# Float64 weights to float32 in three VectorE instructions, and the softmax norm fused with the float16 split

## The chip, the cores and the metric

One NeuronCore of one Trainium2 chip runs the whole program. The metric is the device time of one launch in microseconds (us), from the first to the last instruction on that core. Its engines are TensorE (PE; the loading of its weights is listed apart as PEld), VectorE (DVE), ScalarE (ACT), GpSimd (POOL) and SyncE (SP). SP computes nothing here: it issues every DMA of the kernel.

## The reference

An attention with a window of 128 keys, then two gated blocks on its output. Everything is float32, except that the weights of the two blocks arrive as float64.

```python
# q, k, v: [4, 8, 576, 64]; 8 heads, 576 positions
scores = q @ k^T / 8 - slope[h] * |i - j|, kept for 0 <= i - j < 128
attn = exp(scores - max(scores)); attn = attn / (sum(attn) + 1e-9)
x = (attn @ v)                       # as [2304, 512]
x = ((x @ w_a) * (x @ w_b)) @ w_out      # 512 -> 1536 -> 512
y = ((x @ w1) * (x @ w2)) @ w3 @ w_out2  # 512 -> 1024 -> 1024 -> 512
```

## The kernel before

**Products.** A float32 product is three float32r passes on PE: each operand is split into hi = float32r(x) and lo = x - hi (`split`, L138). The attention's probabilities and v are split in another way, into float16 and bfloat16 parts.

**Weights.** Each piece of a weight (a *part*, 128 x 512 values) is loaded by SP as float64, that is as two 32-bit words for each value (tile `raw`). `convert` (L98) makes float32 of it in stages. Stage s0 takes the absolute value of the high word on ACT (L107). Stage s1 is five DVE instructions: clear what is too small and make a mask (L113), shift and mask (L117), put sign and top bit in (L120), take the exponent (L123), and weigh the low word with it (L127). Stage s3 adds the two on POOL (L132). Then `split` makes hi on ACT (L139) and lo on POOL (L73). There are 76 parts. The tile `ca` holds the value, and the tile `ce`, of which there is one, what comes from the low word; `ce` is also the staging buffer of the product w3 @ w_out2 (L440 to L442). The class `Stages` puts a part's stages into the program in turns, one stage of every live part a turn.

**Attention.** 16 units (a batch and a pair of heads) of 5 query blocks each make 80 steps. A step: scores on PE (L313), bias and minimum on DVE (L325, one for each head), exp with its sum on ACT (L331), sum to reciprocal on DVE (L344, L347), then `probs` (L349): scale by the reciprocal on DVE in place (L357, one for each head), round to float16 on ACT (L363; on DVE, L361, for the first block of a unit), subtract that for the low part on POOL (L73), transpose both parts by a DMA that SP issues (L366), and the product with v on PE (L388) eight steps later. Blocks 1 to 3 of a unit have two heads with 256 keys, block 0 two heads with 128, block 4 one tile of 256.

**After attention.** Ten groups of gated products (L521 and L541 or L559), each with six parts of weights, and 24 parts for the product w3 @ w_out2 between them. From some 285 us on the weights of a group are converted while PE works on the one before.

**Order.** The program is traced through a tile scheduler: it fixes each engine's order of instructions, places the waits, and gives a tile's buffer to the next user when its last reader is through. An engine runs its list in order, so an instruction that waits holds all behind it.

Of the kernel before, what the change touches and what calls it, by code (L numbers as in the profile page):

```python
# [20 lines left out]
# Float32 products run as three float32r passes: an operand x is the exact sum of  # L21
# hi = float32r(x) and lo = x - hi, and x*w = lo*hi' + hi*lo' + hi*hi' to float32's accuracy.
# The second block's w3 @ w_out is formed first: (g @ w3) @ w_out = g @ (w3 @ w_out).
# Weights come as float64: their words are put together as rounded float32 on the chip.
# [6 lines left out]
GROUPS = (6, 4)  # groups of two 128-column chunks of each block's inner features  # L31
TA, TN = 256, 512  # tokens of a tile: beside attention, and after it
HALF = 1280  # the token at which the accumulators are cut in two
LAG, NLAG = 8, 2  # steps of attention from the scores to the product with v, and to the norms
AT = (0, 0, 1, 3)  # steps of a unit at which the next one is transposed
V_AT = {2: 1, 6: 2}  # steps at which the second and the third unit's v are loaded
FILL = 0.75  # microseconds of the first group's products in a step of attention
PACE = (0.3, 0.6)  # turns of the weights' conversion in a step: the first batch, the others
TURN = 400  # tokens of a chunk for each turn later
# [4 lines left out]
def attention_moe_moe(ctx, tc, q, k, v, w_a, w_b, w_o, w_1, w_2, w_3, w_o2, out):  # L44
# [34 lines left out]
    # ---------------------------------------------------------------- weights  # L79
    def load_cols(w, c):  # L80
        """128 columns of a [512, .] weight: [128, 4 * 128] with the rows on 4 x 128 partitions."""
# [7 lines left out]
    def load_rows(w, r, c):  # L89
        """128 rows and 512 columns."""  # L90
# [7 lines left out]
    def convert(raw, hi=None, lo=None, use=()):  # L98
        """Float64's two words as float32, to the nearest (0 below float32's exponents), and its
        split: stages, to be emitted one after the other, each when the one before has run."""  # L100
# [5 lines left out]
        def s0():  # L106
            nc.scalar.activation(a, f32(hw), ACTF.Abs)  # L107

        def s1():
            e = pools["conv"].tile([P, W], F32, name="ce", bufs=1)  # L110
            ei = e.bitcast(I32)
            es.append(e)
            nc.vector.tensor_scalar(  # L113
                out=a, in0=a, scalar1=bits(0x38100000), scalar2=bits(0x3FFFFFF8),
# [639 lines left out]
```

## Time and profile before

| | us |
|---|---|
| median of 3 runs | 1056.13 (1048.25 to 1060.08) |
| profiled execution, first to last instruction | 1056.7 |
| PE busy | 1017.9 (96%) |
| DVE busy | 691.0 (65%) |
| POOL busy | 494.3 (47%) |
| ACT busy | 382.0 (36%) |

The profiled execution has no time of its own beside its span; the span is 0.6 us above the median of the runs. Busy PE is not PE at its peak: its matmuls are pipelined and a waiting one can count as busy. PE's granted clock is a share of 2.4 GHz; 0.5 is 1.2 GHz. A group of instructions is listed as line, engine, operation, out<-in, shape, count | busy us, mean ns of one | idle us of the engine before them and what ended it.

### The profile page before, as it was taken

The page shows a single profiled execution, that of the slowest core. Times are in us where ns is not written, and L with a number is a line of the kernel's source. Part 1 is how long each engine was busy: PE and PEld are TensorE (multiplying, and loading weights), DVE is VectorE, ACT ScalarE, POOL GpSimd, SP SyncE. Part 2 cuts the span into 40 slices and gives each one's busy share as a digit, 9 for nine tenths or more (in the row PEclk, how much of TensorE's full clock was granted, in tenths as well). Part 3 has the DMA queues.
Part 4 walks back from the last instruction along what each step waited for, and adds up shares of the span by engine and source line. Part 5 has one row for each costly group of instructions (what it writes and reads, how often), then busy time and mean ns, then how long its engine had stood idle before and what let it go on. Part 6 is the DMA issues. An engine that isn't in the chain of part 4 may idle for free.

```text
span 1056.7 us, 16482 instructions
## 1 busy us (share of the span) xinstructions
PE 1017.9 (96%) x6162; PEld 838.2 (79%) x6162; DVE 691.0 (65%) x1420; ACT 382.0 (36%) x929; POOL 494.3 (47%) x409
## 2 busy tenths in 40 slices
PE   7889999999999889999999999999999999999998
PEld 5567788787987778887788788888888888888886
DVE  6999997757499995587969659565273373322222
ACT  5555766655344232332333323233322221211110
POOL 6566645445267562264636226477572352421111
PEclk9688979878899899999999999999999999999999
DMA  6867676656333221232232223121021020000012
GB/s 140 170 122 154 118 114 121 123 101 115 81 100 100 79 100 70 74 107 73 99 109 84 77 71 99 60 80 41 1 80 40 20 81 20 20 1 1 11 70 100
DMA packets 160080, 85.23 MB, mean 81 GB/s; under 512 B 128000, under 2 KB 148992, under 8 KB 160000
## 3 DMA queue, kind: packets, MB, share of 16 engines
q1 hardware_dynamic: 160000, 84.18, 31.5%
q8 instruction: 48, 0.79, 0.3%
q14 instruction: 32, 0.26, 0.1%
HBM read 58.20 MB, written 8.91 MB: 64 GB/s over the span
## 4 chain that ended last, share of the span: by engine, by line
PE 62%; DVE 22%; DMA 6%; issue 6%; ACT 2%; POOL 1%; SPq 1%; DVEq 0%; ACTq 0%; POOLq 0%
PE mm L521 33%; PE mm L559 10%; PE mm L541 7%; DVE ca L117 4%; PE tr L388 4%; PE mm L439 4%; PE s L313 3%; DVE pe L357 3%; DVE ca L120 3%; DVE ca L113 2%; DVE ce L123 2%; DMA pt<-pp 2%; DVE ce L127 2%; DMA raw<-in_moe_w_out 1%; DVE pe L325 1%
## 5 line engine op out<-in xcount | busy, mean ns | idle before, releaser
L73 POOL TENSOR_TENSOR gl<-g,gh 128x512 fp32r<-128x512 f32 (+1 forms) x108 | 127.7, 1183 | 265.3 <-ACT gh L531 258.4
L132 POOL TENSOR_TENSOR ca<-ca,ce 128x512 f32<-128x512 f32 x76 | 104.7, 1378 | 138.2 <-DVE ce L127 127.4
L528 DVE TENSOR_TENSOR g<-a,mm 128x512 f32<-128x512 f32 (+1 forms) x108 | 64.1, 594 | 157.3 <-PE mm L521 146.7
L531 ACT ACTIVATE gh<-g 128x512 fp32r<-128x512 f32 (+1 forms) x108 | 60.4, 559 | 209.4 <-DVE g L528 209.1
L73 POOL TENSOR_TENSOR pp<-pe,pp 128x512 f16<-128x512 f32 (+1 forms) x80 | 81.8, 1030 | 73.1 <-ACT pp L363 39.9
L521 PE MATMUL mm<-x_hi,wlA 128*128 128x512 f32 (+1 forms) x464 | 109.2, 356 | 0.0
L521 PE MATMUL mm<-x_lo,whA 128*128 128x512 f32 (+1 forms) x464 | 106.9, 351 | 0.0
L521 PE MATMUL mm<-x_hi,whA 128*128 128x512 f32 (+1 forms) x464 | 106.2, 349 | 0.0
L521 PE MATMUL mm<-x_hi,wlB 128*128 128x512 f32 (+1 forms) x400 | 99.8, 371 | 5.5 <-DVE g L528 5.0
L526 ACT ACTIVATE a<-mm 128x512 f32<-128x512 f32 (+1 forms) x108 | 56.1, 519 | 126.6 <-PE mm L521 126.5
L521 PE MATMUL mm<-x_lo,whB 128*128 128x512 f32 (+1 forms) x400 | 98.8, 369 | 0.0
L521 PE MATMUL mm<-x_hi,whB 128*128 128x512 f32 (+1 forms) x400 | 98.7, 369 | 0.0
L521 PEld LDWEIGHTS mm<-x_lo,whA 128*128 128x128 f32 x464 | 80.3, 197 | 10.5
L521 PEld LDWEIGHTS mm<-x_hi,whA 128*128 128x128 f32 x464 | 79.7, 196 | 11.1
L113 DVE TENSOR_SCALAR ca<-ca 128x512 f32<-128x512 f32 x76 | 48.8, 642 | 60.4 <-ACT ca L107 60.4
L521 PEld LDWEIGHTS mm<-x_hi,wlA 128*128 128x128 f32 x464 | 78.6, 195 | 12.1 <-issue 0.6
L107 ACT ACTIVATE ca<-raw 128x512 f32<-128x512 f32 x76 | 50.9, 669 | 101.5 <-DMA raw<-in_moe_w 51.6
L521 PEld LDWEIGHTS mm<-x_hi,wlB 128*128 128x128 f32 x400 | 70.6, 188 | 19.9 <-DVE g L528 6.1
L117 DVE SCALAR_TENSOR_TENSOR ca<-raw,ca 128x512 int32<-128x512 int32 x76 | 82.4, 1084 | 1.6
L357 DVE TENSOR_SCALAR pe<-pe,st 128x256 f32<-128x256 f32 (+1 forms) x144 | 81.5, 602 | 1.3
L331 ACT ACTIVATE pe<-pe,st 128x256 f32<-128x256 f32 (+1 forms) x144 | 68.7, 478 | 37.6 <-DVE st L325 36.0
L120 DVE SCALAR_TENSOR_TENSOR ca<-raw,ca 128x512 int32<-128x512 int32 x76 | 80.9, 1065 | 1.5
(100 smaller groups left out, 2086.7 us busy)
## 6 DMA issues: line engine op xcount, KB each, us to landing
raw<-in_moe_w SPq DMA_DIRECT2D x32, 512.0 KB, 3.5
raw<-in_moe_w_out SPq DMA_DIRECT2D x20, 512.0 KB, 3.5
raw<-in_moe_w_a SPq DMA_DIRECT2D x12, 512.0 KB, 3.5
raw<-in_moe_w_b SPq DMA_DIRECT2D x12, 512.0 KB, 3.5
out<-acc SPq DMA_DIRECT2D x18, 256.0 KB, 2.0
q_raw<-in_q SPq DMA_DIRECT2D x32, 128.0 KB, 2.6
k_raw<-in_k SPq DMA_DIRECT2D x32, 128.0 KB, 2.8
v_raw<-in_v SPq DMA_DIRECT2D x32, 128.0 KB, 2.6
```

The costliest lines, as they stand in the source:

```text
L73: eng.tensor_tensor(out=out, in0=a, in1=b, op=ALU.subtract)
L113: nc.vector.tensor_scalar(out=a, in0=a, scalar1=bits(0x38100000), scalar2=bits(0x3FFFFFF8), op0=ALU.is_ge, op1=ALU.mult,)
L117: nc.vector.scalar_tensor_tensor(out=ai, in0=hw, scalar=3, in1=ai, op0=ALU.logical_shift_left, op1=ALU.bitwise_and)
L120: nc.vector.scalar_tensor_tensor(out=ai, in0=hw, scalar=-(1 << 30), in1=ai, op0=ALU.bitwise_and, op1=ALU.bitwise_or)
L132: nc.gpsimd.tensor_tensor(out=a, in0=a, in1=es[0], op=ALU.add)
L331: nc.scalar.activation(pe[:, j, :n], pe[:, j, :n], ACTF.Exp, bias=st[:, 0, j:j + 1], scale=-1.0, accum_out=st[:, 1, j:j + 1],)
L357: nc.vector.tensor_scalar(out=pe[:, j, :n], in0=pe[:, j, :n], scalar1=st[:, j:j + 1], scalar2=None, op0=ALU.mult)
L521: nc.tensor.matmul(p, w[:, z, kk, :], x[:, kk, o], start=(y == 0), stop=(y == len(terms) - 1))
L528: nc.vector.tensor_tensor(out=gg, in0=a, in1=ps[1], op=ALU.mult)
L531: nc.scalar.activation(gh, gg, ACTF.Copy)
L541: nc.tensor.matmul(p, w, x, start=(y == 0), stop=(y == len(terms) - 1))
L559: nc.tensor.matmul(p, x, w, start=(y == 0), stop=(y == len(terms) - 1))
```

## The change

Conversion: the part of the low word is now made on ACT, in stage s0, by a copy with a scale into an integer tile `ce` (L111 of the new file), so `ce` is claimed there and no longer by the fourth DVE instruction. Stage s1 is three DVE instructions: maximum with a constant (L115), shift and mask in one instruction with two operations (L118), sign and top bit (L122). Stage s3 is an integer add on POOL (L127) in the place of a float add.

Softmax: the rounding to float16 takes the reciprocal as its scale (ACT, L358, one for each head; on DVE, L354, for block 0), and one DVE instruction for each head (L360) multiplies again, subtracts the rounded value and writes the low part. The scale in place on DVE, the cast L361 and POOL's subtraction are gone.

```diff
         def s0():
             nc.scalar.activation(a, f32(hw), ACTF.Abs)
+            e = pools["conv"].tile([P, W], I32, name="ce", bufs=1)
+            es.append(e)
+            nc.scalar.activation(e, lw, ACTF.Copy, scale=2.0 ** -29)
 
         def s1():
-            e = pools["conv"].tile([P, W], F32, name="ce", bufs=1)
-            ei = e.bitcast(I32)
-            es.append(e)
             nc.vector.tensor_scalar(
-                out=a, in0=a, scalar1=bits(0x38100000), scalar2=bits(0x3FFFFFF8),
-                op0=ALU.is_ge, op1=ALU.mult,
-            )
-            nc.vector.scalar_tensor_tensor(
-                out=ai, in0=hw, scalar=3, in1=ai, op0=ALU.logical_shift_left, op1=ALU.bitwise_and
+                out=a, in0=a, scalar1=bits(0x38000000), scalar2=None, op0=ALU.max
             )
+            nc.vector.tensor_scalar(
+                out=ai, in0=ai, scalar1=3, scalar2=0x3FFFFFF8,
+                op0=ALU.logical_shift_left, op1=ALU.bitwise_and,
+            )
             nc.vector.scalar_tensor_tensor(
                 out=ai, in0=hw, scalar=-(1 << 30), in1=ai, op0=ALU.bitwise_and, op1=ALU.bitwise_or
             )
-            nc.vector.tensor_scalar(
-                out=ei, in0=ai, scalar1=-(1 << 23), scalar2=None, op0=ALU.bitwise_and
-            )
-            nc.vector.scalar_tensor_tensor(
-                out=e, in0=lw, scalar=2.0 ** -52, in1=e, op0=ALU.mult, op1=ALU.mult
-            )
 
         def s3():
-            nc.gpsimd.tensor_tensor(out=a, in0=a, in1=es[0], op=ALU.add)
+            nc.gpsimd.tensor_tensor(out=ai, in0=ai, in1=es[0], op=ALU.add)
...
         for j in range(nj):
-            nc.vector.tensor_scalar(
-                out=pe[:, j, :n], in0=pe[:, j, :n], scalar1=st[:, j:j + 1], scalar2=None, op0=ALU.mult
+            if i == 0:
+                nc.vector.tensor_scalar(
+                    out=pp[:, j, 0, :], in0=pe[:, j, :n], scalar1=st[:, j:j + 1], scalar2=None, op0=ALU.mult
+                )
+            else:
+                nc.scalar.activation(pp[:, j, 0, :], pe[:, j, :n], ACTF.Copy, scale=st[:, j:j + 1])
+        for j in range(nj):
+            nc.vector.scalar_tensor_tensor(
+                out=pp[:, j, 1, :], in0=pe[:, j, :n], scalar=st[:, j:j + 1], in1=pp[:, j, 0, :],
+                op0=ALU.mult, op1=ALU.subtract,
             )
-        if i == 0:
-            nc.vector.tensor_copy(out=pp[:, :, 0, :], in_=pe[:, 0:nj, :n])
-        else:
-            nc.scalar.activation(pp[:, :, 0, :], pe[:, 0:nj, :n], ACTF.Copy)
-        sub(nc.gpsimd, pp[:, :, 1, :], pe[:, 0:nj, :n], pp[:, :, 0, :])
```

The rest of the difference is comments, so that the new file's line numbers stand 1 to 6 lower or higher than before: L320 is the old L325, L339 the old L344, L342 the old L347, L134 the old L139, L108 the old L107, L525, L527, L530 and L545 the old L526, L528, L531 and L546. The scheduler orders every engine's list anew.

DVE just behind attention, where group 1's weights are converted. Before, five instructions for each part, with the gated products' L528 between them:

```order
L113 TENSOR_SCALAR ca<-ca 128x512
L117 SCALAR_TENSOR_TENSOR ca<-raw,ca 128x512
L120 SCALAR_TENSOR_TENSOR ca<-raw,ca 128x512
L113 TENSOR_SCALAR ca<-ca 128x512
L123 TENSOR_SCALAR ce<-ca 128x512
L528 TENSOR_TENSOR g<-a,mm 128x256
L117 SCALAR_TENSOR_TENSOR ca<-raw,ca 128x512
L127 SCALAR_TENSOR_TENSOR ce<-raw,ce 128x512
L120 SCALAR_TENSOR_TENSOR ca<-raw,ca 128x512
```

And now three, of which one still reads `raw`:

```order
L115 TENSOR_SCALAR ca<-ca 128x512
L118 TENSOR_SCALAR ca<-ca 128x512
L122 SCALAR_TENSOR_TENSOR ca<-raw,ca 128x512
L115 TENSOR_SCALAR ca<-ca 128x512
L527 TENSOR_TENSOR g<-a,mm 128x256
L118 TENSOR_SCALAR ca<-ca 128x512
L122 SCALAR_TENSOR_TENSOR ca<-raw,ca 128x512
L527 TENSOR_TENSOR g<-a,mm 128x256
```

The same part takes three places in DVE's list instead of five, and DVE no longer writes `ce`.

ACT in the same stretch, with the engines that each instruction waits for. Before:

```order
L107 ACTIVATE ca<-raw 128x512 [waits DMAHW4_49,Activation_49]
L546 ACTIVATE acc_3521<-mm 128x256 [waits PE_49] x4
L526 ACTIVATE a<-mm 128x256 [waits PE_49,Activation_49]
L107 ACTIVATE ca<-raw 128x512 [waits DMAHW5_49,Pool_49]
L139 ACTIVATE whB_5185<-ca 128x512 [waits Pool_49]
L531 ACTIVATE gh<-g 128x256 [waits DVE_49]
```

And now:

```order
L525 ACTIVATE a<-mm 128x256 [waits PE_49,Activation_49]
L108 ACTIVATE ca<-raw 128x512 [waits DMAHW4_49,Pool_49]
L111 ACTIVATE ce<-raw 128x512 [waits Pool_49]
L134 ACTIVATE whB_5138<-ca 128x512
L530 ACTIVATE gh<-g 128x256 [waits DVE_49]
L525 ACTIVATE a<-mm 128x256 [waits PE_49,Activation_49]
L111 ACTIVATE ce<-raw 128x512 [waits Pool_49]
L134 ACTIVATE whB_5161<-ca 128x512
```

The copy L111 waits for POOL's add of the part before, which frees `ce`, and stands ahead of that part's hi (L134) and of the gated products' L530 and L525.

POOL early in attention, before and then now:

```order
L73 TENSOR_TENSOR v_754<-v_753 128x640
L73 TENSOR_TENSOR pp<-pe,pp 128x2x128
L73 TENSOR_TENSOR pp<-pe,pp 128x2x256 x3
L73 TENSOR_TENSOR v_1031<-v_1030 128x640
L73 TENSOR_TENSOR wlA_604<-ca,whA_603 128x512
```

```order
L73 TENSOR_TENSOR v_749<-v_748 128x640
L127 TENSOR_TENSOR ca<-ca,ce 128x512
L73 TENSOR_TENSOR wlA_600<-ca,whA_599 128x512
L73 TENSOR_TENSOR v_1025<-v_raw_96 128x640
L73 TENSOR_TENSOR v_1026<-v_1025 128x640
```

The subtractions for `pp` are no longer in POOL's list; what is left there in attention is v's split, the weights of the first group and the first gated products.

## Rows read from the trace of the kernel before

**Rows 1.** Stages: start:end, length, busy us (instructions) of each engine, PE's clock, DMA.

```profile
50.00:150.00 100.00, 94.17 (x948) 74.21 (x949) 96.56 (x311) 64.20 (x207) 60.73 (x57) 0.84 0.70 130
150.00:285.00 135.00, 131.71 (x1357) 108.87 (x1353) 91.18 (x347) 76.58 (x258) 61.99 (x62) 0.86 0.59 111
285.00:400.00 115.00, 103.88 (x558) 87.70 (x557) 107.80 (x134) 42.48 (x84) 71.40 (x50) 0.97 0.29 91
400.00:630.00 230.00, 226.16 (x1080) 187.37 (x1078) 160.63 (x232) 71.52 (x124) 97.26 (x71) 1.00 0.26 86
```

**Rows 2.** DVE's groups by line and shape, 20 to 150 us.

```profile
L357 DVE TENSOR_SCALAR pe<-pe,st 128x256 f32<-128x256 f32 x54 | 38.0, 737 | 0.4
...
L357 DVE TENSOR_SCALAR pe<-pe,st 128x128 f32<-128x128 f32 x16 | 9.8, 652 | 0.1
...
L117 DVE SCALAR_TENSOR_TENSOR ca<-raw,ca 128x512 int32<-128x512 int32 x6 | 6.6, 1100 | 0.0
...
L120 DVE SCALAR_TENSOR_TENSOR ca<-raw,ca 128x512 int32<-128x512 int32 x6 | 4.9, 811 | 0.0
...
L127 DVE SCALAR_TENSOR_TENSOR ce<-raw,ce 128x512 f32<-128x512 uint32 x6 | 4.5, 750 | 0.0
...
L113 DVE TENSOR_SCALAR ca<-ca 128x512 f32<-128x512 f32 x6 | 3.5, 577 | 0.0
L123 DVE TENSOR_SCALAR ce<-ca 128x512 int32<-128x512 int32 x6 | 2.9, 476 | 0.0
```

**Rows 3.** Groups by line and shape, whole span: nearest prices, and ACT's in attention.

```profile
L331 ACT ACTIVATE pe<-pe,st 128x256 f32<-128x256 f32 x112 | 56.2, 502 | 30.9 <-DVE st L325 30.8
...
L528 DVE TENSOR_TENSOR g<-a,mm 128x512 f32<-128x512 f32 x72 | 49.2, 684 | 137.8 <-PE mm L521 128.8 <-ACT whB L139 2.5 <-POOL ca L132 2.5
...
L363 ACT ACTIVATE pp<-pe 128x512 f16<-128x512 f32 x48 | 29.9, 625 | 19.4 <-DVE pe L357 14.3 <-DMA pt<-pp 4.8
...
L401 DVE SCALAR_TENSOR_TENSOR x_lo<-tr,x_hi 128x128 fp32r<-128x128 f32 x64 | 17.9, 280 | 6.6 <-ACT x_hi L400 6.4
...
L528 DVE TENSOR_TENSOR g<-a,mm 128x256 f32<-128x256 f32 x36 | 14.9, 414 | 19.6 <-PE mm L521 18.0 <-ACT a L526 1.5
```

**Rows 4.** SP's queue in order of time: start, us, queue, line, operation, tiles, count.

```profile
182.94 1.14 SPq L241 DMA_DIRECT2D k_raw<-in_k  x2
...
184.89 2.52 SPq L366 DMA_TRANSPOSE pt<-pp  x2
```

**Rows 5.** The chain of waits from 50 to 150 us, shares by line.

```profile
by line: DVE pe L357 17.6%; PE tr L388 16.7%; PE s L313 15.4%; issue 7.3%; DVE pe L325 5.9%; PE mm L521 5.7%; PE tr L274 4.6%; DVE st L344 3.6%; PE mm L340 3.1%; DMA q_raw<-in_q 2.6%; DVE x_lo L401 2.2%; DVE qkl L279 2.0%; DVE ca L113 2.0%;
```

**Rows 6.** POOL's subtraction for the softmax, from the page's costliest groups.

```profile
L73 POOL TENSOR_TENSOR pp<-pe,pp 128x512 f16<-128x512 f32 (+1 forms) x80 | 81.8, 1030 | 73.1 <-ACT pp L363 39.9
```

**Rows 7.** DVE's groups by line and shape, 150 to 285 us.

```profile
L357 DVE TENSOR_SCALAR pe<-pe,st 128x256 f32<-128x256 f32 x53 | 27.6, 555 | 0.6
```

**Rows 8.** Groups by line and shape, 285 to 400 us.

```profile
L132 POOL TENSOR_TENSOR ca<-ca,ce 128x512 f32<-128x512 f32 x19 | 28.2, 1483 | 18.2 <-DVE ce L127 18.2
L117 DVE SCALAR_TENSOR_TENSOR ca<-raw,ca 128x512 int32<-128x512 int32 x21 | 27.2, 1297 | 0.4
...
L127 DVE SCALAR_TENSOR_TENSOR ce<-raw,ce 128x512 f32<-128x512 uint32 x19 | 18.5, 972 | 0.5
...
L107 ACT ACTIVATE ca<-raw 128x512 f32<-128x512 f32 x21 | 14.1, 673 | 27.7 <-DMA raw<-in_moe_w_out 11.7 <-DMA raw<-in_moe_w_b 6.8 <-DMA raw<-in_moe_w 5.3
...
L73 POOL TENSOR_TENSOR wlB<-ca,whB 128x512 fp32r<-128x512 f32 x6 | 8.8, 1469 | 5.7 <-ACT whB L139 5.7
...
L139 ACT ACTIVATE whB<-ca 128x512 fp32r<-128x512 f32 x6 | 3.8, 631 | 9.9 <-POOL ca L132 9.9
```

**Rows 9.** DVE in order of time: start, us, engine, line, operation.

```profile
321.22 0.69 DVE L127 SCALAR_TENSOR_TENSOR ce<-raw,ce 128x512 f32<-128x512 uint32 x1
...
322.29 1.66 DVE L117 SCALAR_TENSOR_TENSOR ca<-raw,ca 128x512 int32<-128x512 int32 x1
```

**Rows 10.** POOL in order of time, beside the last of these.

```profile
321.99 1.40 POOL L132 TENSOR_TENSOR ca<-ca,ce 128x512 f32<-128x512 f32 x1 [1.09 <-DVE ce L127]
```

## The prediction

> **What bounds the kernel now.** I read the stages first [rows 1]: busy time of each engine between two times. Look for the engine that has no room. From 50 to 150 us that is DVE, 96.56 of 100 us, with PE's clock at 0.84. From 150 us to the end of attention no engine but PE looks full, and a waiting PE counts as busy. From 285 to 400 us DVE is full again, 107.8 of 115 us, and PE is idle for 115 - 103.88 = 11.1 us. From 400 us on PE is full, 226.16 of 230 us; behind that there is nothing for this change to win. Second, the groups of DVE [rows 2, 7, 8]: they say what fills it. The scale of the softmax, L357, is the largest in attention, with a mean of 737 ns for 256 values where 150 us later it is 555 ns. Third, the chain of waits [rows 5] says whether a full engine is also the path: L357 alone has 17.6% of the chain from 50 to 150 us, but PE's lines L388, L313, L521 and L274 have 42% together. So DVE sets the pace there, and not alone. Last, instructions in order of time [rows 9, 10]: why one instruction has two durations. L127 took 0.69 us with POOL idle; L117, of the same kind and size, took 1.66 us when it started 0.3 us into an add on POOL of 1.40 us. So a DVE instruction of these kinds waits behind POOL, and less work on POOL shortens DVE's as well.
>
> **Attention up to 150 us.** Between 20 and 150 us the change takes from DVE [rows 2] all of L357, 38.0 + 9.8 us, and the five conversion instructions of six parts, 6.6 + 4.9 + 4.5 + 3.5 + 2.9 us: 70.2 us. (The casts L361 go as well; I count them at nothing.) It adds one L360 for each head. No row shows it; it reads one float32 and one float16 tile, and its nearest are L528 with 414 ns at 256 values and L401 with 280 ns at 128 [rows 3]: 54 x 0.414 + 16 x 0.280 = 26.9 us. Its bounds are those 414 ns and the 737 ns that L357 takes beside POOL; I take the lower, because POOL loses 81.8 us of subtractions [rows 6], nearly all that it did beside these. L354 for block 0 is 16 x 0.280 = 4.5 us. The three conversion instructions I price as L113, L123 and L120, whose kinds they are: 6 x (0.577 + 0.476 + 0.811) = 11.2 us. Added, 42.6 us; net, DVE is relieved of 27.6 us.
>
> How much of it is time? A unit has nine head tiles, two of them of 128, so 54 + 16 of L357 are 7.8 units in 130 us, 16.7 us each. DVE's share of one is 0.966 x 16.7 = 16.1 us; 27.6 / 7.8 = 3.5 us less makes 12.6 us. The next engines stand close. SP issues ten loads at 0.57 us and five transposes at 1.26 us for a unit [rows 4], 12.0 us. ACT has 0.642 x 16.7 = 10.7 us; it gets seven scaled copies, priced as L331, which has a column operand too, and loses three copies of 512 and a shorter one: 7 x 0.502 - 3 x 0.625 = 1.6 us more, 12.3 us at most [rows 3]. The six extra copies L111 lie in ACT's idle time (L107's kind, 0.67 us). Three engines at 12 to 13 us and a PE that has 42% of the chain will not run at 12.6; I take 14.2 us, 2.5 us less, times 7.8: **20 us**. Ends: 27.6 us if DVE stays the pace maker, and 5 us if PE and SP hold what they have.
>
> **The rest of attention.** From 150 us the same change gives DVE 27.6 - 53 x 0.414 = 5.7 us [rows 7], and DVE had 91.18 of 135 us, so it is no pace maker. What goes is POOL's subtraction, 1.03 us in the mean [rows 6], from each step's way to its transpose, and DVE's waits behind it. I take 1 us for each of 53 / 7 = 7.6 units, **8 us**. Ends: nothing, as SP's 12.0 us and PE are untouched, and 15 us, 2 us a unit.
>
> **Conversion from 285 to 400 us.** L117 and L127 go, 27.2 + 18.5 us [rows 8], and L118 takes L123's place; DVE falls from 107.8 to 62 us. Now the wait that the change adds: there is one `ce`, and ACT claims it in its first stage instead of DVE in its fourth instruction. L111 waits until POOL's add of the part before is done, and behind it in ACT's list stand that part's hi and the gated products' copies. The ring is POOL's add 1.483, L111 at L107's 0.673, L134 at 0.631, POOL's lo 1.469 [rows 8]: 4.26 us a part, where 21 parts in 115 us are 5.5 us now. So 21 parts take 89 us, less than the 104 us that PE is busy, and PE becomes the bound. It can win its 11.1 us of idle time and the 3% that the clock of 0.97 lacks [rows 1], 3.5 us: 14.6 us at most. The first product of a group still waits for all six parts, so I take **10 us**; the other end is nothing. The integer add on POOL has no row; 1.469 us for a subtraction with a float32r output and 1.483 us for the float add [rows 8] say that the kind of value moves it little. I take the float add's; a longer one is the second rival's case.
>
> **From 400 us on.** PE is idle for 3.8 us of 230; I take **2 us**, ends 0 and 3.8.
>
> Sum: 20 + 8 + 10 + 2 = 40 us. The profiled execution's span is 1056.7 us, so 1016.7; it stands 0.6 us above the median, which makes **1016 us**. With all upper ends, 61 us, it is 995.
>
> **A rule against it.** L127 reads two 32-bit tiles in SBUF and took 0.69 us for 512 values [rows 9]; L528, with one of its inputs in PSUM, takes 0.684 us for 512 and 0.414 us for 256 [rows 3]. So the second input in SBUF costs nothing by itself, and 256 values more cost 0.27 us. The Trainium skill (Vector Engine (DVE) Microarchitecture Reference, section "Points that are easy to get wrong") says of this form that with two SBUF sources that are not bfloat16 it "halves throughput". By it L127 would take some 1.2 us with POOL idle, so the trace disagrees; by it the sum would be that of the third rival.
>
> **Rivals.** *Other engines hold attention* (19%). For it: SP's 12.0 us a unit, PE's share of the chain, and that from 150 us on DVE had a third of its time free and a unit was no faster, 135 / 7.6 = 17.8 us with the tail. Against it: L357 is the first line of the chain. Then 7 us before 150, none after, 6 us in conversion: 1043 us.
>
> *The `ce` ring becomes the bound, slower* (7%). Place: ACT's wait in L111. Its price hangs on the integer add. The ring without it is 2.77 us, so at 2.73 us for the add a part takes the 5.5 us of now. Some 42 parts (three groups and the product w3 @ w_out2) are converted before PE has a lead; to eat attention's 28 us and 1% more, the add must take over 3.6 us. At 3.7 us: 42 x 0.97 = 41 us lost against 28 us won, 1069 us. POOL's rows for 128x512 are 1.47 and 1.48 us [rows 8].
>
> *L360 at half pace* (4%). At 256 values it would take 0.27 us more, at 128 half of that: 54 x 0.27 + 16 x 0.135 = 16.7 us of the 27.6 us are gone. L127's 0.69 us speaks against it. 8 us would be left before 150 us and nothing behind it: 8 + 10 + 2 = 20 us, 1036 us.
>
> *The change does what it says and the new order gives it back* (7%): the lists are made anew, and a product or a transpose put behind a late one can cost each group some us; about 1053 us.
>
> The forecast has 63%, its own range being 995 to 1032. The range for 8 in 10 is 994 to 1045: it takes in the first and third rival and leaves out the slower one. A measurement of this kernel tells about 1%, 10.6 us, from no change. Faster than that: 63 + 4 + 15 of the first rival's 19, 82%. Within it: the rest of the first and most of the last, 9%. Slower: 7 + 2, 9%.
>
> **What the profile would show.** DVE's groups: L357 at 256 gone, L360 near 0.41 us, L115 and L118 near 0.5 us. The stages: attention's last step some 28 us earlier, DVE below 85% before 150 us. In conversion, adds on POOL 4.2 to 4.5 us apart instead of 5.5, PE's idle time in 115 us behind attention below 5 us. The prediction is wrong if units still take over 16 us, if POOL's add takes over 2 us, or if ACT's waits in L111 for POOL stand behind PE's waits.

## The result, and the profile after

The changed kernel takes 1024.1 us in the median (1020.4 to 1030.1, 4 runs), the kernel before 1056.6 us (1048.3 to 1060.1, 4 runs). The ratio is 0.974, with a 95% interval of 0.970 to 0.978. The forecast was 1016 us in a range of 994 to 1045, with 82% on faster by over 1%. The sign and the range held; of the forecast 40 us some 32 came, and they did not come from where they were expected. The profiled execution took 1024.7 us, its span is 1022.6 us. Medians and ratios in this document leave out runs more than 1.5% above the fastest of their kernel, which are three of the twelve of e9 below and no others.

Two marks divide the time: the start of the last x_lo of attention, and the end of the span. Before, the mark is at 281.6 us and 775.2 us follow. After, it is at 264.5 us and 758.1 us follow. So in these two executions attention gave 17.1 us and the work behind it 17.1 us; the prediction had 28 and 12.

First the stages, with the columns and the times of [rows 1]:

```profile
50.00:150.00 100.00, 93.77 (x939) 74.06 (x938) 80.96 (x314) 70.35 (x234) 27.21 (x23) 0.79 0.69 134
150.00:285.00 135.00, 129.88 (x1461) 111.40 (x1460) 96.89 (x354) 90.95 (x295) 35.71 (x32) 0.97 0.63 119
285.00:400.00 115.00, 112.38 (x557) 93.97 (x556) 73.12 (x96) 51.14 (x96) 61.74 (x47) 1.00 0.29 95
400.00:630.00 230.00, 230.00 (x1129) 192.90 (x1128) 127.85 (x189) 94.87 (x167) 108.78 (x84) 1.00 0.30 94
```

DVE fell from 96.56 to 80.96 us in the first stage and from 107.8 to 73.12 us in the third; POOL fell from 60.73 to 27.21 us in the first. PE is not free of gaps in the first stage, and in the last its 230.00 of 230 us leave none.

The groups of DVE from 20 to 150 us, which stand in the place of [rows 2]:

```profile
L360 DVE SCALAR_TENSOR_TENSOR pp<-pe,st,pp 128x256 f16<-128x256 f32 x57 | 35.7, 656 | 3.1 <-ACT pp L358 2.8
...
L360 DVE SCALAR_TENSOR_TENSOR pp<-pe,st,pp 128x128 f16<-128x128 f32 x16 | 5.5, 362 | 0.0
...
L354 DVE TENSOR_SCALAR pp<-pe,st 128x128 f16<-128x128 f32 x16 | 4.6, 321 | 5.1 <-DMA pt<-pp 5.1
...
L122 DVE SCALAR_TENSOR_TENSOR ca<-raw,ca 128x512 int32<-128x512 int32 x6 | 4.1, 685 | 0.0
L115 DVE TENSOR_SCALAR ca<-ca 128x512 f32<-128x512 f32 x6 | 3.0, 493 | 5.1 <-ACT ca L108 5.1
L118 DVE TENSOR_SCALAR ca<-ca 128x512 int32<-128x512 int32 x6 | 2.5, 422 | 0.1
```

The new L360 is the dearest, as L357 was, and its mean of 656 ns is far above the 414 ns that the sum took. The three conversion instructions cost 9.6 us, a little under the 11.2 us priced. Why L360 has such a mean is seen in order of time. On DVE (start, us, engine, line, operation, count):

```profile
189.31 2.36 DVE L360 SCALAR_TENSOR_TENSOR pp<-pe,st,pp 128x256 f16<-128x256 f32 x2 [0.34 <-ACT pp L358]
...
194.94 0.88 DVE L360 SCALAR_TENSOR_TENSOR pp<-pe,st,pp 128x256 f16<-128x256 f32 x2 [0.29 <-ACT pp L358]
```

and on POOL at the same time:

```profile
188.75 1.25 POOL L73 TENSOR_TENSOR v<-v_raw 128x640 f32<-128x640 f32 x1 [8.60 <-PE tr L387]
190.08 1.32 POOL L73 TENSOR_TENSOR v<-v 128x640 bf16<-128x640 f32 x1
197.10 0.73 POOL L73 TENSOR_TENSOR gl<-g,gh 128x256 fp32r<-128x256 f32 x1 [5.71 <-ACT gh L530]
```

Two L360 that met the subtractions of v took 2.36 us together, and two with POOL idle 0.88 us. In the whole trace 88 of the 112 L360 with 256 values overlap nothing on POOL and take 477 ns in the mean, 24 do and take 980 ns. The Trainium skill (SBUF — State Buffer, section "SBUF: two separate sides") says that a DVE operation with two inputs in SBUF and a GpSimd operation that reads SBUF exclude each other for a whole instruction, and that the one that starts first has its way. The trace agrees: of the 24, the seven that began ahead of POOL's instruction took 466 to 484 ns, and the 17 that began during one took 1187 ns in the mean, at most 1504 ns.

The chain of waits from 50 to 150 us, as in [rows 5]:

```profile
by line: PE tr L387 21.5%; PE s L308 20.8%; PE mm L520 16.7%; DMA pt<-pp 11.9%; PE tr L269 10.3%; DMA raw<-in_moe_w_b 4.6%; PE mm L335 3.8%; PE mm L540 3.4%; DVE pe L320 1.7%; DVE qkl L274 1.5%; DVE pp L360 1.1%; DVE ca L115 0.8%; issue 0.7
```

DVE's L357 led it with 17.6%. Now PE's lines lead, and the largest other entry is the transpose DMA, 11.9%.

Behind attention the stages are best compared at the same distance from the mark. These are the 115 and the 230 us of [rows 1] moved forward by 17.1 us:

```profile
267.90:382.90 115.00, 111.54 (x612) 96.09 (x612) 79.87 (x102) 57.11 (x110) 70.08 (x53) 1.00 0.32 103
382.90:612.90 230.00, 230.00 (x1120) 192.24 (x1119) 126.75 (x188) 94.82 (x166) 103.22 (x80) 1.00 0.29 92
```

PE's gaps went from 11.1 to 3.5 us and from 3.8 us to none. What PE waited for (engine, line, what it waited for: us, times, longest), in the kernel before from 285 to 400 us:

```profile
PE mm L521 <- DVE g L528: 5.0, 3, 2.5
PE mm L541 <- POOL gl L73: 4.1, 2, 2.4
PE mm L541 <- DVE acc L548: 1.0, 1, 1.0
PE mm L541 <- ACT gh L531: 0.7, 2, 0.4
PE mm L439 <- DVE w3l L433: 0.2, 1, 0.2
```

and in the changed kernel from 267.9 to 382.9 us:

```profile
PE mm L540 <- POOL gl L73: 1.3, 2, 1.1
PE mm L520 <- ACT acc L545: 1.1, 1, 1.1
PE mm L540 <- ACT gh L530: 0.8, 1, 0.8
PE mm L520 <- DVE g L527: 0.2, 1, 0.2
```

None of these rows names a part of the weights that came late. PE waited for its own products' way through DVE and POOL (g, acc, gl), and that way stood behind conversion instructions. Ahead of the longest wait DVE had these, in order of time:

```profile
344.90 1.65 DVE L117 SCALAR_TENSOR_TENSOR ca<-raw,ca 128x512 int32<-128x512 int32 x1
346.58 0.69 DVE L120 SCALAR_TENSOR_TENSOR ca<-raw,ca 128x512 int32<-128x512 int32 x1
347.19 0.68 DVE L528 TENSOR_TENSOR g<-a,mm 128x512 f32<-128x512 f32 x1
```

and PE went on right behind L528:

```profile
347.93 0.74 PE L521 MATMUL mm<-x_hi,wlB 128*128 128x256 f32 x4 [2.50 <-DVE g L528]
```

There are six such waits of 0.7 us or more, 10.2 us together. Each ended with an instruction that stood directly behind one of the conversion in its engine's list: L132 on POOL twice, L120 twice, L123 and L127 on DVE. From 400 to 630 us there is one row over 1 us of this kind in the kernel before, and in the changed kernel none:

```profile
PE mm L439 <- DVE w3l L433: 3.4, 2, 1.8
```

The groups of the conversion, 270 to 385 us, which answer to [rows 8]:

```profile
L127 POOL TENSOR_TENSOR ca<-ca,ce 128x512 int32<-128x512 int32 x21 | 28.4, 1352 | 36.3 <-ACT ce L111 22.4 <-PE mm L520 6.9 <-DVE ca L122 5.6
...
L111 ACT ACTIVATE ce<-raw 128x512 int32<-128x512 uint32 x20 | 13.4, 672 | 13.6 <-POOL ca L127 10.3 <-DMA w<-ce 3.2
```

The integer add costs 1352 ns, no more than the float add's 1483 ns. L111 does wait for it, 10.3 us in this stretch, and PE pays only for the rows of its waits above.

### The profile page after: what moved, and what is told of

It is laid out like the page before. It is cut to its first block, busy times and chain, and to the rows that moved or that the text cites. A ratio compares the mean times of both kernels' runs of the same rounds, so it can differ in the third digit from the quotient of the medians.

```text
span 1022.6 us, 16444 instructions
## 1 busy us (share of the span) xinstructions
PE 996.2 (97%) x6162; PEld 824.3 (81%) x6162; DVE 548.7 (54%) x1284; ACT 435.7 (43%) x1053; POOL 399.1 (39%) x329
## 4 chain that ended last, share of the span: by engine, by line
PE 85%; DMA 8%; DVE 3%; ACT 2%; POOL 1%; issue 1%; SPq 1%; ACTq 0%; DVEq 0%; POOLq 0%
PE mm L520 45%; PE mm L540 13%; PE mm L558 10%; PE tr L387 5%; PE s L308 4%; PE mm L438 4%; DMA pt<-pp 3%; PE tr L269 2%; DMA raw<-in_moe_w_b 1%; DMA raw<-in_moe_w_out 1%; DMA raw<-in_moe_w_a 1%; ACT ca L108 1%; PE mm L430 1%; DVE ca L122 0%; DVE pe L320 0%
## 5 line engine op out<-in xcount | busy, mean ns | idle before, releaser
L73 POOL TENSOR_TENSOR gl<-g,gh 128x512 fp32r<-128x512 f32 (+1 forms) x108 | 124.5, 1153 | 340.5 <-ACT gh L530 340.5
L527 DVE TENSOR_TENSOR g<-a,mm 128x512 f32<-128x512 f32 (+1 forms) x108 | 64.2, 595 | 217.2 <-PE mm L520 207.0
L127 POOL TENSOR_TENSOR ca<-ca,ce 128x512 int32<-128x512 int32 x76 | 100.6, 1323 | 152.5 <-ACT ce L111 70.9
L530 ACT ACTIVATE gh<-g 128x512 fp32r<-128x512 f32 (+1 forms) x108 | 60.2, 558 | 169.5 <-DVE g L527 169.3
L525 ACT ACTIVATE a<-mm 128x512 f32<-128x512 f32 (+1 forms) x108 | 56.1, 521 | 113.6 <-PE mm L520 113.4
L520 PE MATMUL mm<-x_hi,whA 128*128 128x512 f32 (+1 forms) x464 | 103.6, 345 | 0.0
L115 DVE TENSOR_SCALAR ca<-ca 128x512 f32<-128x512 f32 x76 | 44.4, 584 | 91.4 <-ACT ca L108 91.1
L520 PEld LDWEIGHTS mm<-x_hi,wlA 128*128 128x128 f32 x464 | 78.2, 193 | 12.7 <-issue 0.4
L520 PEld LDWEIGHTS mm<-x_lo,whA 128*128 128x128 f32 x464 | 79.4, 195 | 10.9 <-issue 0.4
L108 ACT ACTIVATE ca<-raw 128x512 f32<-128x512 f32 x76 | 50.7, 668 | 78.6 <-DMA raw<-in_moe_w 41.5
L547 DVE TENSOR_TENSOR acc<-acc,mm 128x512 f32<-128x512 f32 (+1 forms) x100 | 62.1, 630 | 38.0 <-PE mm L540 37.7
L520 PEld LDWEIGHTS mm<-x_lo,whB 128*128 128x128 f32 x400 | 71.1, 188 | 12.8
L520 PEld LDWEIGHTS mm<-x_hi,whB 128*128 128x128 f32 x400 | 71.0, 189 | 12.5
L122 DVE SCALAR_TENSOR_TENSOR ca<-raw,ca 128x512 int32<-128x512 int32 x76 | 79.4, 1045 | 1.9
```

The costliest lines, as they stand in the source:

```text
L73: eng.tensor_tensor(out=out, in0=a, in1=b, op=ALU.subtract)
L122: nc.vector.scalar_tensor_tensor(out=ai, in0=hw, scalar=-(1 << 30), in1=ai, op0=ALU.bitwise_and, op1=ALU.bitwise_or)
L127: nc.gpsimd.tensor_tensor(out=ai, in0=ai, in1=es[0], op=ALU.add)
L520: nc.tensor.matmul(p, w[:, z, kk, :], x[:, kk, o], start=(y == 0), stop=(y == len(terms) - 1))
L525: nc.scalar.activation(a, ps[0], ACTF.Copy)
L527: nc.vector.tensor_tensor(out=gg, in0=a, in1=ps[1], op=ALU.mult)
```

## The experiments

The theory at the start: each part of the change works in its own stage, and in attention PE becomes the pace maker. All times are medians; the ratio is to the kernel before on the same chip, with its interval. "Last step" is the mark described above, and "behind" what follows it, both of the profiled execution.

| run | us | ratio | last step | behind |
|---|---|---|---|---|
| both parts (the change) | 1024.1 | 0.974 (0.970 to 0.978) | 264.5 | 758.1 |
| e1 conversion only | 1024.6 | 0.973 (0.970 to 0.977) | 269.3 | 758.7 |
| e2 softmax only | 1041.7 | 0.990 (0.987 to 0.993) | 257.6 | 779.0 |
| e3 add twice | 1036.0 | 0.984 (0.980 to 0.989) | 269.6 | 764.9 |
| e4 no products in attention | 1069.0 | 1.016 (1.012 to 1.020) | 249.4 | 815.9 |
| e5 the change again | 1024.5 | 0.974 (0.967 to 0.980) | 266.5 | 758.2 |
| e6 more warming | 1023.9 | 0.973 (0.968 to 0.978) | 265.7 | 758.2 |
| e7 no warming | 1021.0 | 0.971 (0.966 to 0.976) | 256.4 | 758.0 |
| e8 five buffers | 1017.5 | 0.967 (0.962 to 0.972) | 255.5 | 758.8 |
| e9 before, five buffers | 1050.6 | 0.998 (0.995 to 1.002) | 272.4 | 775.3 |
| e10 conversion, five buffers | 1026.7 | 0.976 (0.972 to 0.979) | 265.8 | 759.2 |
| e11 six buffers | 1024.2 | 0.975 (0.971 to 0.980) | 261.1 | 758.3 |
| e12 five, no warming | 1018.0 | 0.968 (0.965 to 0.971) | 258.0 | 758.8 |

The last column is steady, 758.0 to 759.2 us in nine profiles of eight kernels that have the new conversion as it stands and attention's products in their place. Attention is what moves between executions. A median's last step can so be worked out as the median less "behind" less the 2 us by which a run's time stands over its span: 276 us before (1053.6 us in the last 17 runs), 264 for the change, 264 for e1, 261 for e2, 261 for e7, 257 for e8 and e12, 273 for e9, 264 for e11, 266 for e10. The profiled execution of the kernel before was a late one; by medians attention gave some 12 us, not 17.

**e1, the conversion alone.** From the changed kernel:

```
...
-                nc.scalar.activation(pp[:, j, 0, :], pe[:, j, :n], ACTF.Copy, scale=st[:, j:j + 1])
...
-            nc.vector.scalar_tensor_tensor(out=pp[:, j, 1, :], ...)
+            nc.vector.tensor_scalar(out=pe[:, j, :n], in0=pe[:, j, :n], scalar1=st[:, j:j + 1], ...)
...
+            nc.scalar.activation(pp[:, :, 0, :], pe[:, 0:nj, :n], ACTF.Copy)
+        sub(nc.gpsimd, pp[:, :, 1, :], pe[:, 0:nj, :n], pp[:, :, 0, :])
```

> The changed kernel with the softmax of before (DVE scales, POOL subtracts); only the conversion is new. Markers: attention's last step started at 281.6 us before and 264.5 us with both changes; behind it came 775.2 us before and 758.1 us after. Theory (each part of the change works in its own stage, and in attention PE takes over as the pace maker as soon as DVE has some room): behind attention all of the 17 us come, 758 us give or take 4; in attention a part of the 17 us, since DVE loses 11 of its 27.6 us: last step at 272 to 278 us; total 1056.6 - 17 - 6 = 1033 us. Rival 1 (the late gain comes from the new order of all lists, not from the conversion): behind attention 768 us or more, total above 1043 us. Rival 2 (either part alone already takes DVE from the path, the rest is PE): attention's last step at 264 to 268 us, total 1024 to 1028 us.

Measured: 758.7 us behind the mark, as the theory has it, so rival 1 falls. The last step is at 269.3 us in the profile, a little behind rival 2's bounds, and at 264 us by the median, as early as rival 2 has it. The conversion alone takes the whole gain, 1024.6 against 1024.1 us, where the theory had 1033.

**e2, the softmax alone.** From the changed kernel:

```
...
-            nc.scalar.activation(e, lw, ACTF.Copy, scale=2.0 ** -29)
... the three DVE instructions go, and in their place come the five DVE instructions of the kernel before, the last two writing ce
-            nc.gpsimd.tensor_tensor(out=ai, in0=ai, in1=es[0], op=ALU.add)
+            nc.gpsimd.tensor_tensor(out=a, in0=a, in1=es[0], op=ALU.add)
```

> The changed kernel with the conversion of before (five DVE instructions, ce written by DVE); only the softmax is new. Theory (each part works in its own stage): behind attention nothing is won, 775 us give or take 4; attention's last step at 268 to 274 us; total about 1056.6 - 11 = 1045 us. Rival 1 (the late gain comes from the new order): behind attention 766 us or less, total 1036 us or less. Rival 2 (either part alone takes DVE from the path): last step at 264 to 268 us, total 1040 us.

Measured: behind the mark 779.0 us, so nothing is won there, and the late gain is not the new order's. The last step is 257.6 us in the profile and 261 by the median, earlier than the theory had it. So each part alone brings attention to 261 to 264 us, and the two together bring no more: the parts do not add. At the same distances behind the mark PE has the gaps of the kernel before, 11.7 of 115 us and 5.4 of 230:

```profile
261.00:376.00 115.00, 103.29 (x552) 88.10 (x552) 107.08 (x134) 42.42 (x83) 70.83 (x50) 0.96 0.28 91
376.00:606.00 230.00, 224.62 (x1066) 185.77 (x1066) 158.58 (x231) 70.49 (x122) 95.89 (x70) 0.99 0.27 86
```

**e3, a longer ring through ce.**

```
             nc.gpsimd.tensor_tensor(out=ai, in0=ai, in1=es[0], op=ALU.add)
+            nc.gpsimd.tensor_tensor(out=ai, in0=ai, in1=es[0], op=ALU.add)
```

> The changed kernel with POOL's integer add of each converted part done twice, the second behind the first (so the low words are added twice). A part's ring through ce grows by one add, 1.3 us by the add's mean of 1323 ns: from 4.26 us by the prediction to 5.6 us, about what a part took in the kernel before (115 us for 21 parts). Theory (behind attention the conversion's pace is what the change improved, and with 4.3 us a part PE is just fed): 21 parts x 1.3 us = 27 us more conversion before 400 us, of which PE's reserve takes some; behind attention 770 to 780 us instead of 758, total 1036 to 1050 us, and ACT's L111 waits for POOL in nearly every part. Rival (the parts were fast enough anyway, the gain came from DVE's work being gone): behind attention 758 to 763 us, total below 1031 us.

Measured: 764.9 us behind the mark, between the two expectations; of the 12 us that the total grew, 7 are there and the rest in attention. The first adds of a part came 5.64 us apart, where the changed kernel has 4.22 and the kernel before 5.53 (18 gaps each). A conversion no faster than before's keeps 10 of the 17 us. That L111 would wait for POOL in nearly every part was wrong: 2.2 us in all. POOL itself was busy for 97.5 of 115 us from 273 to 388 us. PE's waits there (without those under 0.5 us) are one, for the first w3 part:

```profile
PE mm L431 <- POOL ca L128: 8.7, 1, 8.7
```

So the pace of the parts is worth at most 7 of the 17 us. That the rest comes with DVE's room is inferred: 10 us stay with the pace gone, and PE's waits for g, acc and w3l above fit it.

**e4, attention without products.**

```
-FILL = 0.75
+FILL = 0.0
```

> The changed kernel with FILL = 0: the gated products of the first group that ran on PE between attention's steps all run behind attention. They took 16.7 us of the chain of 100 us from 50 to 150 us and 23.9 + 8.8% of the 115 us from 150 us to attention's end (lines 520 and 540): about 55 us. Theory (PE is the pace maker of attention after the change): attention's last step some 30 to 50 us earlier, at 215 to 235 us; the products come behind it at full clock, so the total changes by less than 15 us, to 1015 to 1040 us. Rival (SP's issues, ACT or DVE hold attention, PE has room): the last step stays at 255 us or later, and the total grows by what was moved, 30 us or more, to 1055 us or above.

Measured: the total of the rival, and a last step at 249.4 us between the two. 58 us more stand behind attention, and 15 us were won in it. What the theory left out is the clock. From 20 to 150 us and from 150 to 255 us:

```profile
20.00:150.00 130.00, 118.63 (x1066) 87.33 (x1066) 110.60 (x417) 91.39 (x296) 36.74 (x29) 0.64 0.76 152
150.00:255.00 105.00, 91.78 (x967) 71.90 (x967) 75.51 (x313) 65.44 (x223) 17.12 (x14) 0.67 0.66 128
```

With the products gone PE was granted 0.64 and 0.67, and 159 us of attention ran at the half level (1.2 GHz) against 85 us. PE's products went and its clock fell with them, so the run does not tell what PE without products does at the upper level. PE's busy time, 91.78 of 105 us in the second stage, shows that it was not the only one to hold attention here.

**e5 to e7, the clock.** e5 is the changed kernel, unedited. e6 and e7 edit one line:

```
-WARM_UNITS, WARM = 3, 2
+WARM_UNITS, WARM = 6, 4      (e6)
+WARM_UNITS, WARM = 0, 0      (e7)
```

> The changed kernel itself, profiled a second time, to see how far attention's end and TensorE's half level (1.2 GHz) move between executions of one program. First profile: attention's last step at 264.5 us, 85 us of attention at the half level. With the softmax alone it was 257.6 us with 51 us at the half level. Theory (the 7 us between the two lie in what the clock granted in that one execution): the second profile lies elsewhere in the stretch from 257 to 270 us, and earlier where the half level took less. Rival (the conversion's three instructions in the new order slow attention by themselves): 263 to 266 us again, whatever the clock.

Measured: 266.5 us, 2 us later with 61 us at the half level instead of 85. The theory falls, and the rival's 263 to 266 us is nearly met: the half level of an execution does not say when attention ends.

> The changed kernel with four warming products behind each product with v in the first six units, not two in the first three: their results go nowhere. Theory (PE is the pace maker of attention since the change, and what it still loses there it loses to the half level, 75 of the first 155 us): half-level time in attention falls from 85 us to 50 us or less and the last step comes 3 to 12 us earlier, total 1012 to 1022 us. Rival (PE is bound by its own instructions, the added products only take room): half level little changed, last step 5 to 15 us later, total 1028 to 1040 us.

Measured: nothing, 1023.9 us; 61 us at the half level, as in e5 without the added products. Neither expectation holds.

> The changed kernel without warming products in the units (two behind each product with v in the first three units are left out; the ten ahead of attention stay). Theory (the clock decides): more half level before 80 us, last step 0 to 6 us later, total 1024 to 1031 us. Rival (PE's own instructions decide; the warming products cost 24 x 0.21 us at the full level and did not keep the level up, since 58 of the 68 us from 9 us on were at the half level): last step 3 to 8 us earlier, total 1016 to 1021 us.

Measured: 85 us at the half level, 55 of them in one piece from 39 to 94 us, and still the last step 256.4 us in a profile that was this kernel's fastest run (1016.6 us), 261 us by the median. The rival's direction, at the edge of what can be told: its interval overlaps that of the change.

**e8, the loop through pt.**

```
-        pp = sm_p.tile([P, 2 * 2 * 2 * P], F16, name="pp", bufs=4)...
+        pp = sm_p.tile([P, 2 * 2 * 2 * P], F16, name="pp", bufs=3)...
...
-        t = sm_p.tile([P, 8 * P], F16, name="pt", bufs=4)...
+        t = sm_p.tile([P, 8 * P], F16, name="pt", bufs=5)...
... and the same for the tile of the warming products, which shares the name pt
```

> The changed kernel with five buffers for the transposed weights of attention (pt) and three for those ahead of the transpose (pp), not four and four. After the change SP's transposes wait 75 us between 20 and 265 us for PE to give back a pt buffer. Theory (PE is the pace maker and SP's waits only follow it): nothing is won, last step at 260 to 269 us, total within 6 us of 1024. Rival (a transfer of 3 to 5 us that starts only when a buffer comes free holds the product with v; DMA pt<-pp has 12 to 14% of the chain): last step 5 to 15 us earlier, total 1009 to 1019 us.

Measured: the rival. The last step is 9 us earlier in the profile and 7 by the medians, the total 1017.5 us. A transpose is issued 7.5 us behind its norm instead of 10.6 us (mean of steps 46 to 78). The gain comes late: the 40th of the 80 norms (L342) started at 132.3 us, where the two profiles of the change have 132.5 and 130.3 us, and the 80th at 242.4 us, where they have 251.9 and 253.9 us. The chain from 50 to 150 us in e8:

```profile
by line: PE s L308 19.4%; PE tr L387 17.6%; PE mm L520 16.9%; DVE pp L360 9.7%; DMA pt<-pp 9.3%; PE tr L269 9.0%; issue 4.1%; PE mm L540 2.9%; PE mm L335 2.0%; DVE pe L320 1.8%; ACT pp L358 1.0%; DVE qkl L274 1.0%; ACT pe L326 0.8%; DVE x_l
```

The transpose DMA has less of it, DVE's L360 comes back with 9.7%, and no time is won: the limits stand close together. From 150 to 250 us the chain of the changed kernel is

```profile
by line: PE mm L520 20.9%; PE tr L387 20.5%; PE s L308 16.8%; DMA pt<-pp 13.9%; PE mm L540 10.1%; PE tr L269 7.4%; DVE pp L354 2.4%; DVE pp L360 2.1%; DVE st L339 2.0%; DVE pe L320 1.7%; ACT pe L326 0.5%; DVE qkl L274 0.5%; issue 0.4%; DVE 
```

and that of e8

```profile
by line: PE tr L387 28.6%; PE mm L520 24.8%; PE s L308 18.2%; PE mm L540 12.8%; PE tr L269 5.7%; DMA pt<-pp 5.0%; DVE pp L360 1.6%; ACT pe L326 1.1%; DVE pe L320 0.7%; issue 0.5%; DVE qkl L274 0.5%; DVE x_lo L400 0.3%; DVE st L339 0.2%; DVE
```

Here the transpose DMA falls from 13.9% to 5.0%. The granted clock does not explain it: 0.96 in the change, 0.95 in e8.

**e9 and e10, the same buffers without the new softmax.** The edit is e8's, on the kernel before and on e1.

> The kernel before, with pt in five buffers and pp in three, as the run with five transposed buffers had them. There it brought 9 us of attention. Theory (the kernel before was held by DVE, which has L357 as the first line of its chain; the loop through pt's buffers became the pace maker only when DVE had room): at most 3 us, last step at 278 to 284 us, total within 4 us of the kernel before. Rival (the loop through pt held the kernel before as well, and DVE's relief was never what counted): last step 6 us or more earlier, at 275 us or before, total 6 to 10 us below the kernel before.

Measured: 0.998 (0.995 to 1.002), no difference clear of the noise, and no decision. The median is 3 us lower, at the theory's limit, and the interval leaves room for a gain of 6 us. The profile speaks for the rival: last step at 272.4 us, the 80th norm at 259.1 us where the kernel before has 268.7, and the transpose DMA, 10.8% of the chain from 150 to 250 us before, is not in its chain there. But the profile of the kernel before was a late one.

> The new conversion alone (softmax of before), with pt in five buffers and pp in three. Conversion alone reached the whole change's time, 1024.6 us. Theory (with four buffers either part of the change takes attention to the floor that the loop through pt sets, some 262 to 266 us, and the softmax part counts once that floor is lowered): here last step 262 to 268 us, total 1020 to 1026 us, 3 to 8 us above the whole change with five buffers (1017.5 us). Rival (the softmax part is worth nothing in either case): last step at 254 to 258 us, total 1015 to 1019 us.

Measured: 1026.7 us, just above the theory's bounds, and a last step of 265.8 us within them; the rival falls. One buffer more is worth nothing here (e1 has 1024.6 us). Without the new softmax DVE still leads the chain from 50 to 150 us:

```profile
by line: DVE pe L353 14.2%; PE mm L517 11.2%; PE tr L384 9.7%; PE s L308 9.4%; DMA pt<-pp 7.3%; DVE pe L320 6.6%; DVE st L339 5.5%; issue 4.5%; PE tr L269 4.0%; ACT pe L326 3.6%; DVE qkl L274 3.5%; DVE x_lo L397 2.5%; DVE ca L122 2.1%; PE m
```

That DVE's lead is the reason is not shown: from 150 to 250 us, where e8 has its gain, L353 has 4.4% of this kernel's chain and the transpose DMA 15.3%. The softmax part, worth nothing beside the conversion with four buffers (1024.6 and 1024.1 us), is worth 9 us with five (1026.7 and 1017.5 us).

**e11 and e12, further.** e11 sets pt to six buffers and pp and pe to three; e12 is e8 with e7's line.

> The changed kernel with pt in six buffers, and pp and pe in three instead of four. With pt in five and pp in three it was 1017.5 us, last step at 255.5 us. Theory (the loop through pt: each buffer more lets a transfer of 3 to 5 us start a step earlier, and the second one more brings less than the first): last step at 250 to 255 us, total 1012 to 1017 us. Rival (five were enough, PE's own instructions are the floor, or pe in three holds the scores): last step at 255 to 262 us, total 1017 to 1024 us.

Measured: the rival, at its upper edge, 1024.2 us. Whether pe's missing buffer took it or the sixth pt brings nothing is not separated.

> The changed kernel with pt in five buffers, pp in three, and no warming products in the units. The first alone gave 1017.5 us and the second 1021.0 us, against 1024.1 us. Theory (both give PE room in the first units, the warming products by 24 x 0.21 us and more at the half level): last step at 249 to 253 us, total 1010 to 1015 us. Rival (without warming the half level comes back and eats it): last step at 255 us or later, total 1016 to 1022 us.

Measured: the rival's total, 1018.0 us, nothing on top of e8. e8 and e12 are the fastest kernels here: nine of their ten runs took 1014.5 to 1019.4 us (one 1022.5), and the six runs of the change 1020.4 to 1030.1.

**Still open.** Every edit makes the lists of all engines anew, and that alone may move attention. From 150 us on a unit takes 15.0 and 15.3 us in the two profiles of the change, and 13.5 to 14.0 us in those of e2, e6, e7, e8, e11 and e12, of which e2, e6 and e7 have four pt buffers; e6 and e7 do the same work as the change there. Two of the six are their kernel's fastest run (e7, e11), which takes part of it. How much of e8's 7 us is the buffer and how much the order was not tried. That the buffer counts rests on the totals of e8 against the change and of e12 against e7, 7 and 3 us; that it counts only once DVE has room rests on e10 and is left open by e9. And nothing here shows what holds attention up to 150 us: from 20 to 150 us a unit takes 15.2 to 16.4 us in all ten profiles with the new softmax, whatever their buffers, products and warming products.

## Why the prediction was right, and where not

**Attention up to 150 us, 20 us forecast: mis-sized.** The 40th of the 80 norms came at 139.6 us before and at 132.5 us after, 130.3 us in the second profile of the change: 7 to 9 us by then. Two choices failed.

The price of L360. "I take the lower, because POOL loses 81.8 us of subtractions [rows 6], nearly all that it did beside these": POOL kept the subtractions of v, 20.3 us of its 38.8 us from 20 to 150 us:

```profile
L73 POOL TENSOR_TENSOR v<-v 128x640 bf16<-128x640 f32 x8 | 10.2, 1277 | 0.6
L73 POOL TENSOR_TENSOR v<-v_raw 128x640 f32<-128x640 f32 x8 | 10.1, 1259 | 42.3 <-PE tr L387 31.3 <-DMA v_raw<-in_v 8.6 <-DMA pt<-pp 2.4
```

At the bound's lower end L360 would cost 26.9 us (26.8 by the factors given); at the measured means the same counts cost 54 x 0.656 + 16 x 0.362 = 41.2 us. That takes 14 us from the relief of 27.6 us. Half of it came back where the sum counted nothing: DVE's other instructions took 52.8 us for 38 steps before (122.97 us busy less the 70.2 us that go) and 51.5 us for 42 steps after (106.93 less 41.2, 4.6 and 9.6), 6.8 us less for as many steps. Two entries make up most of it: L339, 291 ns in the mean where L344 took 405 ns, and the casts L361, 2.3 us, which the sum put at nothing.

The pace. DVE's work per unit did fall to what was forecast, 106.93 of 130 us at 15.4 us a unit being 12.7 us against 12.6. But a unit took 15.4 and 15.2 us, not 14.2 (17.3 before, counted by norms between 20 and 150 us). With DVE out of the way, PE's lines have 76.5% of the chain from 50 to 150 us, and the transpose DMA has 11.9%, against less than 2% in the row shown of before. "Three engines at 12 to 13 us" weighed busy times and left out such waits: a transpose waits until PE has given a pt back. Which of them keeps a unit at 15.4 us stays open. A fifth pt buffer does not change it (15.5 us in e8), nor does leaving out the products (15.3 us in e4, at the lower clock) or the warming (15.6 us in e7).

The sum also took the two parts of the change as one relief. e1 and e2 show that either alone brings attention to 264 and 261 us by the medians, and both together to 264 us: beyond what one part gives, the relief was worth nothing with four pt buffers.

**The rest of attention, 8 us forecast:** 6 to 10 us, the last of the 80 norms being 16.8 and 14.8 us early in the two profiles. Here the size held in the profiles; by the medians, with 12 us for all of attention, 3 to 5 us would be left for this part. The argument was a shorter way to the transpose, and SP's queue shows that this came: what it waited for ahead of a transpose from 20 to 255 us, before (line, what it waited for: us, times, longest),

```profile
SPq L366 <- PE tr L388: 33.2, 17, 4.3
SPq L366 <- POOL pp L73: 19.2, 21, 1.6
SPq L366 <- POOL v L73: 15.6, 18, 1.4
```

and after:

```profile
SPq L365 <- PE tr L387: 33.6, 24, 3.5
SPq L365 <- PE s L308: 29.2, 23, 5.8
SPq L365 <- PE tr L269: 8.4, 6, 2.3
```

POOL is gone from these, and other lines of PE have taken its place. The forecast also leaned on units that were no faster from 150 us on, 17.8 us "with the tail"; counted by norms they took 16.0 us there, against 17.3 us up to 150 us.

**Conversion, 10 us forecast, and from 400 us on, 2 us: 17 us in all.** The adds on POOL are 4.22 us apart, against 4.26 worked out and 5.53 before; PE's gaps fell to 3.5 us and the clock of 0.97 became 1.00. These markers held, and still the mechanism was half wrong. "The first product of a group still waits for all six parts" was the reason to take 10 of 14.6 us, and PE's waits do not name parts, but DVE's and POOL's results for PE's own products. e3 bears it out: with parts 5.64 us apart 10 of the 17 us stay. DVE did not fall to the 62 us forecast, but to 79.87 of 115 us, because L118 and L122 met POOL's instructions and took 1028 and 1160 ns in the mean. By the copies of the gated products (L525, 108 in each kernel), the gain is 8.6 us at 90 us behind the mark, 11.8 us at 147 us, 17.8 us at 306 us, and 16.6 us at the last one. The last 5 us fall to the stage that was given 2 us. With both upper ends, 14.6 + 3.8 us, that part of the sum would have been 18.4 us.

**The rivals.** *Other engines hold attention* was right in its number up to 150 us, where it had 7 us, and wrong behind it, where it had nothing. *The ce ring* did not decide: the add costs 1.35 us. e3 also shows the rival's price too high. With two adds of 1.45 and 1.41 us, past the 2.73 us at which it has a part take as long as before, the kernel kept 10 us behind attention and was still 1.6% faster than before. ACT waited in L111 for POOL for 2.2 us only: POOL's own list more than ACT's claim set the pace. *L360 at half pace*: its 0.68 us at 256 values is near the mean of 656 ns, and the cause is not its own; with POOL idle two took 0.88 us. That row also speaks against the rule quoted for it (the Trainium skill, Vector Engine (DVE) Microarchitecture Reference, "Points that are easy to get wrong"). *The new order gives it back* cannot be excluded for some us from 150 us on.

So the direction was right and for the stage behind attention the reason in part, but that the total came so near is luck: two errors of opposite sign, by the two profiles 10.9 us too much in attention and 5.1 us too little behind it, leave 5.8 of the 8 us between 1016 and 1024. The other 2 us are the step from span to time: a run takes some 2 us longer than its span, and the prediction took 0.6 us off. By the medians attention's error is 16 us, and about half of it is taken back by the 5 us behind attention and by the kernel before, which was 2.5 us faster in its later runs (1053.6 us) than the prediction's 1056.1 us.

## What to carry over

Price an instruction that shares SBUF with POOL by the row of its free time and by the row beside POOL, and count which POOL work stays, not which goes. When one engine is relieved, look for a loop through few buffers (here four of pt, with a DMA of 3 to 5 us in it) before dividing busy time by units, and do not expect two reliefs of the same engine to add. Where PE has gaps in a stage whose weights are converted beside it, read what PE waited for: a busy conversion costs through the products' own copies, and the conversion's pace may be the smaller part of the price.

## What was not expected of the hardware

The integer add of 128x512 on POOL took 1352 ns in the conversion behind attention, where the float add of the kernel before took 1483 ns. ACT turned the unsigned low words into scaled integers in 672 ns, its absolute value of the same shape took 669 ns. 85 and 61 us of attention at TensorE's half level, in two executions of one program, ended attention at 264.5 and 266.5 us; and 99 us of it in e12 at 258.0 us. An instruction of DVE with one input is held by POOL as well: L118 (int32, 128x512) took 426 ns in the mean in 35 cases that overlap nothing on POOL, and 1148 ns in the 41 that do.
